# A list schedule with a shared port, a clock and a load pipe, a rank for each unit of work, and 1e-9 as a column of the sum

## The chip, the core and the metric

The kernel runs on one core of one Trainium2 chip. The metric is the device time of one execution in microseconds, the median over several runs. A profiled execution has a span besides, from the first to the last instruction that the profiler records; the device time is a little longer than the span.

The core's engines run side by side, each with its own queue of instructions in program order: PE (TensorE, matmuls), DVE (VectorE), ACT (ScalarE), POOL (GpSimd) and SP, which here only issues transfers between the chip's memory and the on-chip buffers. An instruction starts when those ahead of it on its engine allow it and the semaphores that it waits for are there. So the order within each queue is fixed when the program is built.

## The reference

Sparse attention of 8 batches, 8 heads, 576 positions and 64 columns per head feeds a gated layer of 512 columns:

```python
scores = scale * np.matmul(q, k.transpose(0, 1, 3, 2))
mask_local = (rel >= 0) & (rel < stride)                  # stride = 32, heads 0 to 3
mask_strided = (rel >= 0) & (pos[None, :] % stride == pos[:, None] % stride)   # heads 4 to 7
scores = np.where(masks[None, :, :, :], scores, -1000000000.0)
scores = scores - np.max(scores, axis=-1, keepdims=True)
attn = np.exp(scores)
attn = attn / (np.sum(attn, axis=-1, keepdims=True) + 1e-09)
x = np.matmul(attn, v)                                    # heads side by side: (8, 576, 512)
xp = np.concatenate([np.zeros((B, K - 1, D)), x], axis=1)
for k in range(K):                                        # K = 5
    gate_pre += conv_w[k][None, None, :] * xp[:, k:k + S, :]
gate = 1.0 / (1.0 + np.exp(-gate_pre))
val = x @ w_val
return (gate * val @ w_out).astype(np.float32)
```

The three weights arrive as float64; the kernel gets their bits and makes float32 values of them on the chip.

## The kernel before, in words

**Units of work.** For each batch b there are: three units of local attention (L, u = 0 to 2, two blocks of 96 positions each), two of strided attention (S, u = 0 and 1), four splits of x into a high and a low part (X, one per 128 columns), four gates (G, one per 128 columns), eight value groups (V, four times 128 columns e in two halves hf of the 576 positions, 12 matmuls each, of high and low parts) and four or five projection groups (P, 128 rows each, 12 matmuls). A local unit goes so: scores on PE into one of two banks `s_ps`; the mask added and the rows' maximum taken on DVE; maximum subtracted on POOL; exponential on ACT (tile `SML`, or `SMS` for strided units); sum, addition of 1e-9 and reciprocal on DVE (columns of a small tile `ST`); multiplication on POOL into `PB`; transposes on PE; copies on ACT into `BDL`; matmuls with v on PE into `x_ps`; a copy on ACT into `xs`. The strided unit multiplies into `PS`, transposes on DVE (`PT`) and copies into `BDS` on ACT. In batch 0's local units PE adds the mask by a matmul, and DVE subtracts the maximum. There are four gate tiles for all batches: DVE makes the gate's convolution in four steps per tile, ACT the tanh, and for batch 0's first gate PE makes the convolution. After the value group DVE multiplies gate and value into `GV`, ACT and POOL make its high and low part `ghi` and `glo`, and the projection reads these.

**Weights.** w_val comes in four parts of 512 KB into the tiles `xs`, w_out in four parts into one tile `osb2` (so each w_out load can start only when DVE has read the part before). Each part takes four passes on DVE (TENSOR_SCALAR, three SCALAR_TENSOR_TENSOR, in the gate tiles for w_val and `w64` for w_out), two on ACT and one subtraction on POOL. The conv weights take four small steps on DVE.

**The planner.** The program isn't issued as it is written. Class `Plan` records each step with its engine, an estimated cost, a rank and the steps that it depends on, which it finds from overlapping tiles. `issue` then makes a list schedule: it takes the engine that can start earliest, and on it the step of lowest rank among those that are ready by the planner's clock, and calls the instruction there (line 140, so nearly every instruction of the program has line 140 in the profile). The estimated costs are formulas of the operand's size, and between engines the constants `LATENCY` and `TURN` are added. A rank is 100 times the batch plus a number from the tables `RL`, `RS`, `RG`, `RV`, `RP` (one number per batch), `RWL`, `RWV`, `RWO` (one per weight part) and `RZ`. Up to 40 us of planned time the planner puts idle matmuls on zeros into PE's gaps (line 255). Memsets are on line 265.

The three lines that the softmax ends with:

```python
dve(rank, V.tensor_reduce, out=st[:, 1, :n], in_=sm, axis=AX.X, op=ALU.add)
dve(rank, V.tensor_scalar, out=st[:, 1, :n], in0=st[:, 1, :n], scalar1=1e-9, scalar2=None, op0=ALU.add)
dve(rank, V.reciprocal, extra=0.052, out=st[:, 2, :n], in_=st[:, 1, :n])
```

Of the kernel before, what the change touches and what calls it, by code (L numbers as in the profile page):

```python
# [21 lines left out]
KC = 5  # L22
# [11 lines left out]
class Plan:  # L34
# [6 lines left out]
    def __init__(self, filler, until):  # L41
        self.filler, self.until, self.spare = filler, until, None
        self.steps = []
        self.writes = {}
        self.reads = {}
# [16 lines left out]
    def add(self, engine, cost, rank, calls):  # L62
# [22 lines left out]
        self.steps.append((engine, cost, rank, calls, deps))  # L85
        return i

    def issue(self):
# [7 lines left out]
        free = {"pe": 1.1, "pool": 1.07, "dve": 0.9, "act": 1.9, "sp": 1.68}  # L96
        open_ = {}
        for i, s in enumerate(steps):
            if not left[i]:
                open_.setdefault(s[0], []).append(i)  # L100
        done = 0
        end = 0.0
        live, clear = {}, {}
        while done < len(steps):
            best = None
            for engine, queue in open_.items():
                if not queue:
                    continue
                t0 = free.get(engine, 0.0)
                start = max(t0, min(ready[i] for i in queue))  # L110
                if best is None or start < best[0]:
                    best = (start, engine)
            start, engine = best
# [3 lines left out]
            _, cost, _, calls, _ = steps[pick]  # L117
            t0 = free.get(engine, 0.0)
            free[engine] = start + cost
            over = start + cost + self.LATENCY[engine]  # L120
            end = max(end, over)
            for j in users[pick]:
                same = steps[j][0] == engine
                ready[j] = max(ready[j], start + cost + self.TURN[engine] if same else over)
                left[j] -= 1
                if not left[j]:
                    open_.setdefault(steps[j][0], []).append(j)
            if engine == "pe" and start < self.until:
                idle = [t for t in self.spare if not live.get(t.name) and clear.get(t.name, 0.0) <= t0]
                if idle:  # L130
                    for _ in range(int((start - t0 - 0.1) / (0.216 if t0 > COLD else 0.45))):
                        self.filler(idle[0])
            if engine == "pe":
                live[calls[0][1]["out"].name] = len([j for j in users[pick] if steps[j][0] != "pe"])
            else:
                for name in {ap.name for _, kw in calls for ap in kw.values() if hasattr(ap, "name")}:
                    if name in live:
                        live[name] -= 1
                        clear[name] = max(clear.get(name, 0.0), over)
            got = [fn(**kw) for fn, kw in calls]  # L140
            LOG.append((engine, start, cost, steps[pick][2], calls, got, pick))
            done += 1
# [4 lines left out]
def tile_sparse_attention_moe(  # L147
# [20 lines left out]
    plan = Plan(None, WARM)  # L168
# [19 lines left out]
    def dve(rank, fn, fast=False, extra=0.0, **kw):  # L188
        n = max(size(kw[k]) for k in ("out", "in0", "in_") if k in kw)
        plan.add("dve", ((n / 2 if fast else n) + 66) / 960.0 + extra, rank, [(fn, kw)])  # L190

    def act(rank, fn, wait=0.0, **kw):
        plan.add("act", size(kw["out"]) / 1200.0 + 0.05 + wait, rank, [(fn, kw)])

    def gps(rank, fn, two=True, extra=0.0, **kw):
        plan.add("pool", size(kw["out"]) * (2.35 if two else 1.03) / 1200.0 + 0.07 + extra, rank, [(fn, kw)])

    def pe(rank, each, calls):
        plan.add("pe", each * len(calls), rank, calls)
# [4 lines left out]
    def load(rank, out, in_):  # L204
        n = out.ap[0][1] * size(out)
        plan.add("sp", max(n * 4 / 360e3, 0.5), rank, [(nc.sync.dma_start, dict(out=out, in_=in_))])
# [56 lines left out]
    def zero(engine, rank, ap):  # L263
        eng = V if engine == "dve" else G
        plan.add(engine, size(ap) / (960.0 if engine == "dve" else 1200.0) + (0.02 if engine == "dve" else 0.035), rank, [(lambda out: eng.memset(out, 0.0), dict(out=ap))])

    def keep(rank, ap, step, base, sign):
        gps(rank, G.affine_select, False, extra=0.067, out=ap, in_=ap, pattern=[[step, ap.ap[1][1]]], compare_op=ALU.is_ge,
            fill=NEG, base=base, channel_multiplier=sign)

    for j in range(2):
        zero("dve", -9, KBL[:, j, :, :])
    zero("dve", -9, qSs[:, 2 * S:])


    zero("pool", -9, maskL[:, :])
    zero("pool", -9, maskS[:, :])
    for g in range(4):
        keep(-9, maskL[32 * g:32 * g + 32, :], 1, -1, -1)
        keep(-9, maskL[32 * g:32 * g + 32, :], -1, 32, 1)  # L280
    gps(-9, G.tensor_copy, False, extra=0.6, out=maskF[:, :, :], in_=maskL[:, None, :].to_broadcast([P, 3, 64]))
    plan.add("pool", 0.1, -9, [(lambda out: G.memset(out, NEG), dict(out=maskF[0:64, 0, 0:32]))])
# [345 lines left out]
```

## Time and profile before

| what | us (MB in the last row) |
|---|---|
| median of 3 runs | 349.1 (348.87 to 351.06) |
| the profiled execution | 349.0 |
| its span | 347.2 |
| PE busy | 313.3 (90%) |
| DVE busy | 261.3 (75%) |
| ACT busy | 222.8 (64%) |
| POOL busy | 211.1 (61%) |
| bytes read from and written to HBM | 33.84 and 9.44 MB |

How to read it: the rows with shares give the time in which each engine had an instruction running. A busy PE isn't PE at its peak, since a matmul at a lower clock is busy for longer; the clock that was granted stands in the windows' column PEclk (1.00 is full). In a group of instructions the columns are line, engine, operation, output and inputs with their sizes, the count, then busy time and mean nanoseconds of one, then the idle time just before them and what ended it. In a row of the timeline the start and the duration come first, and brackets give the idle time before it and what ended it. A wait's row gives the sum, how often, and the longest.

### The profile page before, as it was taken

The page shows a single profiled execution, that of the slowest core. Times are in us where ns is not written, and L with a number is a line of the kernel's source. Part 1 is how long each engine was busy: PE and PEld are TensorE (multiplying, and loading weights), DVE is VectorE, ACT ScalarE, POOL GpSimd, SP SyncE. Part 2 cuts the span into 40 slices and gives each one's busy share as a digit, 9 for nine tenths or more (in the row PEclk, how much of TensorE's full clock was granted, in tenths as well). Part 3 has the DMA queues.
Part 4 walks back from the last instruction along what each step waited for, and adds up shares of the span by engine and source line. Part 5 has one row for each costly group of instructions (what it writes and reads, how often), then busy time and mean ns, then how long its engine had stood idle before and what let it go on. Part 6 is the DMA issues. An engine that isn't in the chain of part 4 may idle for free.

```text
span 347.2 us, 9442 instructions
## 1 busy us (share of the span) xinstructions
PE 313.3 (90%) x3851; PEld 264.6 (76%) x3856; DVE 261.3 (75%) x447; ACT 222.8 (64%) x469; POOL 211.1 (61%) x248
## 2 busy tenths in 40 slices
PE   6879469788986999999999999999998999899995
PEld 2456358677875887898878988888898889888984
DVE  7786699999998599669837992979799945976200
ACT  7368666867857758547597747597469735764221
POOL 8676568878838835837458922976387805581510
PEclk9869989989999999999999999999999999999999
DMA  7965947625066406510456013923341031002012
GB/s 270 310 181 184 312 142 223 192 80 163 33 184 201 140 30 167 203 46 25 175 150 205 2 62 127 325 73 85 124 140 45 25 114 42 1 26 97 2 60 91
DMA packets 23419, 43.88 MB, mean 126 GB/s; under 512 B 3088, under 2 KB 13072, under 8 KB 22800
## 3 DMA queue, kind: packets, MB, share of 16 engines
q1 hardware_dynamic: 23376, 43.28, 39.5%
q8 instruction: 30, 0.49, 0.6%
q14 instruction: 13, 0.11, 0.1%
HBM read 33.84 MB, written 9.44 MB: 125 GB/s over the span
## 4 chain that ended last, share of the span: by engine, by line
PE 43%; DVE 26%; ACT 12%; POOL 8%; issue 5%; DMA 4%; SPq 1%; POOLq 0%; ACTq 0%; DVEq 0%
PE m_ps L140 35%; DVE gate L140 12%; DVE ST L140 7%; PE x_ps L140 4%; POOL PB L140 3%; PE s_ps L140 3%; ACT BDS L140 3%; DMA KBS<-in_kS_dram 3%; POOL xlo L140 3%; ACT BDL L140 2%; DVE w L140 2%; ACT gate L140 2%; PE t_ps L140 2%; DMA KBL<-in_kL_dram 2%; POOL PS L140 2%
## 5 line engine op out<-in xcount | busy, mean ns | idle before, releaser
L140 DVE SCALAR_TENSOR_TENSOR gate<-xs,cw,gate 128x576 f32<-128x576 f32 x124 | 126.0, 1035 | 10.4 <-ACT gate L140 9.3
L140 PE MATMUL m_ps<-xhi,wv 128*128 128x288 f32 x512 | 107.3, 303 | 4.9 <-DVE GV L140 4.9
L140 PE MATMUL m_ps<-wo,ghi 128*128 128x512 f32 x288 | 89.5, 392 | 0.0
L140 PEld LDWEIGHTS m_ps<-xhi,wv 128*128 128x128 f32 x512 | 82.0, 189 | 8.7 <-DVE GV L140 6.0
L140 POOL TENSOR_TENSOR glo<-GV,ghi 128x288 fp32r<-128x288 f32 x64 | 60.7, 956 | 43.3 <-ACT ghi L140 42.7
L140 PE MATMUL m_ps<-xlo,wv 128*128 128x288 f32 x256 | 76.0, 297 | 0.0
L140 POOL TENSOR_TENSOR xlo<-xs,xhi 128x576 fp32r<-128x576 f32 x32 | 49.5, 1564 | 27.7 <-ACT xhi L140 15.3
L140 PEld LDWEIGHTS m_ps<-wo,ghi 128*128 128x128 f32 x288 | 53.3, 188 | 11.0
L140 PE MATMUL m_ps<-wo,glo 128*128 128x512 f32 x144 | 56.4, 391 | 0.0
L140 PEld LDWEIGHTS m_ps<-xlo,wv 128*128 128x128 f32 x256 | 48.5, 189 | 0.0
L140 ACT CAST ghi<-GV 128x288 fp32r<-128x288 f32 x64 | 27.3, 432 | 24.6 <-DVE GV L140 24.2
L140 DVE SCALAR_TENSOR_TENSOR GV<-gate,m_ps 128x288 f32<-128x288 f32 x64 | 28.2, 441 | 13.5 <-PE m_ps L140 11.8
L140 ACT ACTIVATE gate<-gate 128x576 f32<-128x576 f32 x31 | 21.3, 686 | 26.4 <-DVE gate L140 26.3
L140 POOL TENSOR_TENSOR PB<-SML,ST 128x256 f32<-128x256 f32 (+1 forms) x48 | 30.4, 647 | 10.6 <-DVE ST L140 6.8
L140 ACT COPY xs<-x_ps 128x288 f32<-128x288 f32 (+1 forms) x56 | 32.0, 597 | 7.4 <-PE x_ps L140 7.4
L140 ACT ACTIVATE osb<-m_ps 128x512 f32<-128x512 f32 x36 | 21.0, 592 | 18.2 <-PE m_ps L140 16.1
L140 ACT COPY BDL<-t_ps 64x256 f32<-64x256 f32 (+1 forms) x72 | 26.6, 370 | 8.3 <-PE t_ps L140 7.3
L140 PEld LDWEIGHTS m_ps<-wo,glo 128*128 128x128 f32 x144 | 27.0, 188 | 6.2 <-POOL glo L140 0.6
L140 ACT COPY BDS<-PT 32x288 f32<-32x288 f32 x64 | 27.7, 433 | 5.6 <-DVE PT L140 4.6
L140 DVE TENSOR_REDUCE ST<-SML 128x6 f32<-128x384 f32 x45 | 24.1, 540 | 6.7 <-ACT SML L140 6.3
L140 PE MATMUL x_ps<-BDS,vSs 128*64 128x72 f32 x512 | 21.4, 236 | 5.5 <-ACT BDS L140 4.6
L140 PEld LDWEIGHTS x_ps<-BDS,vSs 128*64 128x64 f32 x512 | 18.5, 142 | 10.0 <-ACT BDS L140 6.1
(83 smaller groups left out, 421.0 us busy)
## 6 DMA issues: line engine op xcount, KB each, us to landing
out_dram<-osb SPq DMA_DIRECT2D x36, 256.0 KB
qLs<-in_qL_dram SPq DMA_DIRECT2D x16, 288.0 KB
KBL<-in_kL_dram SPq DMA_DIRECT2D x16, 288.0 KB
vLs<-in_vL_dram SPq DMA_DIRECT2D x8, 576.0 KB
qSs<-in_qS_dram SPq DMA_DIRECT2D x16, 288.0 KB
KBS<-in_kS_dram SPq DMA_DIRECT2D x16, 288.0 KB
vSs<-in_vS_dram SPq DMA_DIRECT2D x32, 128.0 KB
xs<-in_w_val_dram SPq DMA_DIRECT2D x4, 512.0 KB
```

What stands on the lines that cost most here:

```text
L140: got = [fn(**kw) for fn, kw in calls]
```

## The change

It has three parts.

**The planner's model.** `LATENCY` and `TURN` go. A step on DVE or POOL that uses the port which both share now waits for the other engine's last such step, less `PORT`. PE has a clock: in windows of 3.413 us its busy share decides whether the next matmuls count 1.9 times as long. A load takes 0.6 on SP, and its bytes go through one pipe for all loads at 330 KB per us. On ACT a step whose output begins on another partition than the one before begins after that one's end. An engine is free again a little before a step's end (`EARLY`). The steps' costs are new numbers. No instruction is added by this part, except that the number of idle matmuls comes from it.

**Ranks.** Every unit of work has a name (`L3.1`, `V1.2.0`, `load qS4`, `make wo2`), 270 in all, and one number in the table `RANK`. The old tables go. `ONPE` names the same three units as before, and `HELD` is empty, so its branch isn't taken.

**1e-9.** `SML` is 65 columns wide instead of 64, `SMS` 19 instead of 18; four memsets on POOL write 1e-9 into the added columns once; the sum runs over the wide tile; and the 40 additions on DVE go (24 of 6 columns, 16 of 16).

```diff
-    LATENCY = {"pe": 0.2, "dve": 0.15, "act": 0.14, "pool": 0.1, "sp": 0.95}
-    TURN = {"pe": 0.0, "dve": 0.12, "act": 0.15, "pool": 0.1, "sp": 0.0}
+    AFTER = {"pe": 0.045, "dve": 0.05, "act": 0.05, "pool": 0.04, "sp": 0.05}
+    EARLY = {"pe": 0.07, "dve": 0.08, "act": 0.1, "pool": 0.04, "sp": 0.0}
+    PORT = {"dve": 0.19, "pool": 0.14}
+    WINDOW, QUIET, BUSY, SLOW = 3.413, 0.48, 0.85, 1.9
+    ISSUE, TO_DATA, TO_END = 0.6, 1.2, 0.65
...
-            pick = min((i for i in queue if ready[i] <= start + 1e-9), key=lambda i: (steps[i][2], i))
+            pick = min((i for i in queue if ready[i] <= start + 1e-9), key=lambda i: (rank[steps[i][2]], i))
...
+            if engine == "pe":
+                fill = 0
+                idle = [t for t in self.spare if not live.get(t.name) and clear.get(t.name, 0.0) <= t0]
+                if idle and start < WARM:
+                    fill = max(0, int((start - t0 - 0.1) / (0.216 if warm else 0.45)))
+                    for _ in range(fill):
+                        self.filler(idle[0])
+                now = int(start / self.WINDOW)
+                spent = fill * (0.216 if warm else 0.45)
+                while window < now:
+                    full = min(1.0, (busy + min(spent, self.WINDOW)) / self.WINDOW)
+                    spent = max(0.0, spent - self.WINDOW)
+                    warm = full >= self.QUIET if warm else full >= self.BUSY
+                    window, busy = window + 1, max(0.0, busy - self.WINDOW)
...
+            elif engine == "sp":
+                free[engine] = start + self.ISSUE
+                pipe = max(pipe, start + self.TO_DATA) + took
+                done = pipe + self.TO_END
+            else:
+                if where != part[engine]:
+                    start = max(start, over[engine] + 0.015)
+                part[engine] = where
+                done = start + took
+                if shared:
+                    wait = max(0.0, port - start - self.PORT[engine])
+                    done += wait
+                    port = done
+                free[engine] = done - early
...
-    SML = Ring(tiles(2, [P, 2, 3, 64], "SML"))
+    SML = Ring(tiles(2, [P, 2, 3, 65], "SML"))
-    SMS = Ring(tiles(2, [P, 16, NT], "SMS"))
+    SMS = Ring(tiles(2, [P, 16, NT + 1], "SMS"))
...
+    for t in SML.items:
+        zero("pool", "zero SML", t[:, :, :, 64:65], 1e-9)
+    for t in SMS.items:
+        zero("pool", "zero SMS", t[:, :, NT:], 1e-9)
...
+        sm = whole[:, :, :w]
...
-        dve(rank, V.tensor_reduce, out=st[:, 1, :n], in_=sm, axis=AX.X, op=ALU.add)
-        dve(rank, V.tensor_scalar, out=st[:, 1, :n], in0=st[:, 1, :n], scalar1=1e-9, scalar2=None, op0=ALU.add)
-        dve(rank, V.reciprocal, extra=0.052, out=st[:, 2, :n], in_=st[:, 1, :n])
+        dve(group, V.tensor_reduce, out=st[:, 1, :n], in_=whole, axis=AX.X, op=ALU.add)
+        dve(group, V.reciprocal, extra=0.0055 * n, out=st[:, 2, :n], in_=st[:, 1, :n])
...
-RL = [-25.55, -293.34, -91.63, -48.77, -38.39, -126.5, -119.7, -85.3]
+RANK = [
+    53, 94, 159, 161, 120, 116, 124, 125, 131, 160, 39, 99, 216, 3, 158, 28, 228, 70, 82, 152, 80, 201, 34, 249,
```

**Where instructions move.** The new line of the issuing call is 171 instead of 140. The first place is DVE's start. `gate0` and `gate1` hold the weight part in work, `xs0` and `xs1` its raw bits (parts 0 and 1 in `xs0`, 2 and 3 in `xs1`); `s_ps` are batch 0's first scores. Before:

```order
L140 TENSOR_SCALAR gate1_93<-xs0_77 128x512
L140 SCALAR_TENSOR_TENSOR gate1_93<-xs0_77,gate1_93 128x512 x2
L140 TENSOR_SCALAR gate0_92<-xs0_77 128x512
L140 SCALAR_TENSOR_TENSOR gate1_93<-gate3_95,gate1_93 128x512
L140 SCALAR_TENSOR_TENSOR gate0_92<-xs0_77,gate0_92 128x512 x2
L140 SCALAR_TENSOR_TENSOR gate0_92<-gate2_94,gate0_92 128x512
L265 MEMSET xs0_77 128x4x4
L140 TENSOR_REDUCE ST0_108<-s_ps0_117 128x6
L140 TENSOR_TENSOR SML0_102<-s_ps0_117,ST0_108 128x3x2x64
```

and in the change, from part 1's last pass on:

```order
L171 SCALAR_TENSOR_TENSOR gate1_93<-gate3_95,gate1_93 128x512
L171 TENSOR_SCALAR gate0_92<-xs1_78 128x512
L171 TENSOR_SCALAR w640_115<-cw64_91 128x20
...
L171 TENSOR_SCALAR gate1_93<-xs1_78 128x512
...
L171 SCALAR_TENSOR_TENSOR cw_90<-w641_116,w640_115 128x20
L171 SCALAR_TENSOR_TENSOR gate1_93<-gate3_95,gate1_93 128x512
L171 TENSOR_SCALAR w640_115<-osb2_114 128x512
L171 TENSOR_REDUCE ST0_108<-s_ps0_117 128x6
L171 TENSOR_REDUCE ST1_109<-s_ps1_118 128x6
```

All four parts of w_val and the conv weights now stand ahead of the first reduction of scores; before, two parts did. On PE 65 idle matmuls stand ahead of the first scores instead of 16, and 25 later in both, so 90 in all instead of 41.

The second place is DVE in the middle of batch 1's softmaxes, between passes over w_out in `w640`. Before:

```order
L140 TENSOR_REDUCE ST1_109<-SML1_103 128x6
L140 TENSOR_REDUCE ST2_110<-SML0_102 128x6
L140 TENSOR_SCALAR ST1_109<-ST1_109 128x6
L140 TENSOR_TENSOR SMS0_106<-s_ps0_117,maskS_66 128x288
L140 RECIPROCAL ST1_109<-ST1_109 128x6
L140 TENSOR_SCALAR ST2_110<-ST2_110 128x6
L140 TENSOR_REDUCE ST0_108<-SMS0_106 128x16
L140 RECIPROCAL ST2_110<-ST2_110 128x6
```

and in the change:

```order
L171 SCALAR_TENSOR_TENSOR w640_115<-w641_116,w640_115 128x512
L171 TENSOR_REDUCE ST1_109<-SML1_103 128x6
L171 RECIPROCAL ST1_109<-ST1_109 128x6
L171 STREAM_TRANSPOSE PT0_101<-PS1_100 128x512
L171 TENSOR_REDUCE ST2_110<-SML0_102 128x6
L171 TENSOR_TENSOR SML1_103<-s_ps1_118,maskL_64 128x3x2x64
L171 RECIPROCAL ST2_110<-ST2_110 128x6
L171 TENSOR_TENSOR SMS0_106<-s_ps0_117,maskS_66 128x16x18
```

The reciprocal follows the sum without an addition between. The row that writes `SMS0` is batch 1's first strided unit S1.0 in both; in the change 14 instructions stand between the last pass that reads part wo1 out of `osb2` and this row.

The third place is SP's queue of loads. Before:

```order
L140 DMA osb2_114<-in_w_out_dram 128x4x256
L140 DMA qLs_71<-in_qL_dram 64x1152 x2
L140 DMA KBL_73<-in_kL_dram 64x2x576 x2
L140 DMA osb2_114<-in_w_out_dram 128x4x256
L140 DMA vLs_75<-in_vL_dram 96x6x256
L140 DMA vLs_75<-in_vL_dram 32x5x256
L140 DMA qSs_72<-in_qS_dram 64x1152 x2
L140 DMA KBS_74<-in_kS_dram 64x1152 x2
```

and in the change:

```order
L171 DMA qLs_71<-in_qL_dram 64x1152
L171 DMA KBL_73<-in_kL_dram 64x2x576 x2
L171 DMA osb2_114<-in_w_out_dram 128x4x256
L171 DMA vSs_76<-in_vS_dram 2x2048 x2
L171 DMA qLs_71<-in_qL_dram 64x1152
L171 DMA vSs_76<-in_vS_dram 2x2048
L171 DMA qSs_72<-in_qS_dram 64x1152
L171 DMA KBS_74<-in_kS_dram 64x1152 x2
L171 DMA osb2_114<-in_w_out_dram 128x4x256
L171 DMA qSs_72<-in_qS_dram 64x1152
```

The two halves of a load of q were neighbours; now a part of w_out and other loads stand between them, three times in the program: for batch 1's local and strided q and for batch 3's local q.

More of the change, by code (lines that the diff above doesn't have):

```diff
@@ L60, in _meet, with add @@
         return a[0] < b[1] and b[0] < a[1] and a[2] < b[3] and b[2] < a[3]
-    def add(self, engine, cost, rank, calls):
+    def add(self, engine, took, group, calls, port=False, early=None, part=0):
         i = len(self.steps)
@@ L84, in add, with issue @@
             self.writes.setdefault(name, []).append((i, boxes))
-        self.steps.append((engine, cost, rank, calls, deps))
+        self.steps.append((engine, took, group, calls, deps, port, self.EARLY[engine] if early is None else early, part))
         return i
-    def issue(self):
+    def issue(self, rank):
         steps = self.steps
@@ L103, in issue @@
+        port = pipe = end = 0.0
+        warm, window, busy = True, 0, 0.0
         live, clear = {}, {}
[L104 to L113, printed above, removed]
+        for _ in steps:
+            start, engine = min((max(free[e], min(ready[i] for i in open_[e])), k) for k, e in enumerate(self.ENGINES) if open_[e])
+            engine = self.ENGINES[engine]
@@ L114, in issue @@
             queue = open_[engine]
-            pick = min((i for i in queue if ready[i] <= start + 1e-9), key=lambda i: (steps[i][2], i))
+            pick = min((i for i in queue if ready[i] <= start + 1e-9), key=lambda i: (rank[steps[i][2]], i))
             queue.remove(pick)
[L117 to L121, printed above, removed]
+            _, took, _, calls, _, shared, early, where = steps[pick]
@@ L122, in issue @@
+            over[engine] = done
+            end = max(end, done)
             for j in users[pick]:
-                same = steps[j][0] == engine
-                ready[j] = max(ready[j], start + cost + self.TURN[engine] if same else over)
+                ready[j] = max(ready[j], done + (0.035 if steps[j][0] == engine else self.AFTER[engine]))
                 left[j] -= 1
                 if not left[j]:
[L127 to L132, printed above, removed]
+                    open_[steps[j][0]].append(j)
@@ L138, in issue @@
                         live[name] -= 1
-                        clear[name] = max(clear.get(name, 0.0), over)
+                        clear[name] = max(clear.get(name, 0.0), done)
             got = [fn(**kw) for fn, kw in calls]
-            LOG.append((engine, start, cost, steps[pick][2], calls, got, pick))
-            done += 1
+            LOG.append((engine, start, took, steps[pick][2], calls, got, pick))
         return end
@@ L261, in tile_sparse_attention_moe, with zero @@
     make_identity(nc, ident)
[L263 removed]
+    def zero(engine, group, ap, value=0.0):
         eng = V if engine == "dve" else G
[L265 to L268 removed]
+        plan.add(engine, size(ap) / (1170.0 if engine == "dve" else 1200.0) + 0.1, group,
+                 [(lambda out: eng.memset(out, value), dict(out=ap))])
@@ L269, in keep @@
+    def keep(group, ap, step, base, sign):
+        gps(group, G.affine_select, 0.001, extra=0.17, out=ap, in_=ap, pattern=[[step, ap.ap[1][1]]], compare_op=ALU.is_ge,
             fill=NEG, base=base, channel_multiplier=sign)
     for j in range(2):
[L272 to L277, printed above, removed]
+        zero("dve", "zero KBL", KBL[:, j, :, :])
+    zero("dve", "zero KBL", qSs[:, 2 * S:])
+    zero("pool", "mask L", maskL[:, :])
@@ L278, in tile_sparse_attention_moe @@
+    zero("pool", "mask L", maskS[:, :])
     for g in range(4):
[L279 to L282, printed above, removed]
-    act(-9, A.copy, out=maskLB[:, :], in_=maskL[:, :])
-    act(-9, A.copy, out=maskFB.rearrange("p k w -> p (k w)"), in_=maskF.rearrange("p k w -> p (k w)"))
@@ L314, in from_f64 @@
+        dve(group, V.scalar_tensor_tensor, out=t if whole is None else whole, in0=u, scalar=LEAST, in1=t,
             op0=ALU.is_ge, op1=ALU.mult)
```

314 lines of the change are left out of this document (166 added, 148 removed), and 11 rows, old and new, of the table RANK.

## The prediction

> **What bounds the kernel now.** I read the page of the profile first, then the busy time of each engine in stretches, then the waits of PE and DVE, and last the groups of instructions that the change touches.
>
> ```profile
> span 347.2 us, 9442 instructions
> PE 313.3 (90%) x3851; PEld 264.6 (76%) x3856; DVE 261.3 (75%) x447; ACT 222.8 (64%) x469; POOL 211.1 (61%) x248
> PE 43%; DVE 26%; ACT 12%; POOL 8%; issue 5%; DMA 4%; SPq 1%; POOLq 0%; ACTq 0%; DVEq 0%
> ```
>
> PE is busy for 90% of the span, yet the chain that ended last runs through DVE for 26%. Two engines bound the kernel at different times. The stretches show where one hands over to the other; their bounds are the first scores (9.24), the middle of the attention of the first batches (54.6), the first value group of batch 1 that is behind everything (111.7), and the last stretches of PE.
>
> ```profile
> core 0: us, PE busy (x) PEld busy (x) DVE busy (x) ACT busy (x) POOL busy (x), PEclk, DMA share, GB/s
> 0.00:9.24 9.24, 6.03 (x16) 2.11 (x17) 6.99 (x13) 7.14 (x12) 8.03 (x24) 1.00 0.79 276
> 9.24:54.60 45.36, 34.91 (x663) 24.64 (x668) 35.89 (x73) 28.03 (x64) 30.83 (x35) 0.85 0.73 217
> 54.60:111.70 57.10, 47.08 (x730) 40.85 (x725) 55.67 (x96) 42.82 (x94) 41.81 (x46) 0.97 0.51 158
> 111.70:145.40 33.70, 31.56 (x328) 26.99 (x325) 27.87 (x45) 24.01 (x51) 21.35 (x26) 1.00 0.43 135
> 145.40:329.70 184.30, 179.94 (x2065) 158.98 (x2066) 134.42 (x222) 117.42 (x247) 107.78 (x120) 1.00 0.28 90
> 329.70:347.20 17.50, 13.77 (x62) 11.06 (x60) 0.45 (x1) 3.42 (x6) 1.26 (x2) 1.00 0.20 75
> ```
>
> From 54.6 to 111.7 DVE is busy for 55.67 of 57.10 us and PE for 47.08 with 0.97 of its clock: DVE bounds. From 111.7 on PE is busy for 31.56 of 33.70 and then 179.94 of 184.30, and DVE has room: PE bounds. The hand-over is seen in single rows:
>
> ```profile
> 109.97 0.56 DVE L140 TENSOR_TENSOR SML<-s_ps,maskL 128x384 f32<-128x384 f32 x1
> 110.58 0.77 PE L140 MATMUL s_ps<-KBS,qSs 128*32 128x36 f32 x64 [1.49 <-DVE SML L140]
> 111.70 0.51 PE L140 MATMUL m_ps<-xhi,wv 128*128 128x288 f32 x2
> ```
>
> PE waits 1.49 us until DVE has read a score bank, writes batch 3's strided scores, and begins the value group of batch 1 (gate tile 2, first half) that I call M. From here PE hardly stops. So the time is that of M plus what PE has left, and the time of M is what DVE must do ahead of it, plus DVE's idle time. DVE was busy for 6.99 + 35.89 + 55.67 = 98.55 us by then, and idle for 111.70 - 98.55 = 13.15.
>
> **Term A: DVE's work ahead of M.** I counted DVE's instructions ahead of M's place in both orders. The change has 11 additions of 1e-9 on 6 columns and 7 on 16 columns less (those of this part of the program; the other 22 lie where PE bounds), and the new order has 2 steps of the gate's convolution, one transpose, one sum over SMS and 2 reciprocals of 16 columns fewer, but 2 reductions of SML, one GV and one reciprocal of 6 more.
>
> ```profile
> L140 DVE SCALAR_TENSOR_TENSOR gate<-xs,cw,gate 128x576 f32<-128x576 f32 x124 | 126.0, 1035 | 10.4 <-ACT gate L140 9.3
> L140 DVE TENSOR_SCALAR ST<-ST 128x6 f32<-128x6 f32 x24 | 12.3, 512 | 0.2
> L140 DVE TENSOR_SCALAR ST<-ST 128x16 f32<-128x16 f32 x16 | 4.3, 270 | 0.1
> L140 DVE STREAM_TRANSPOSE PT<-PS 128x512 f32<-128x512 f32 x16 | 11.3, 706 | 6.2 <-POOL PS L140 5.6 <-ACT BDS L140 0.3
> L140 DVE TENSOR_REDUCE ST<-SMS 128x16 f32<-128x288 f32 x32 | 13.9, 442 | 3.9 <-ACT SMS L140 3.6
> L140 DVE TENSOR_REDUCE ST<-SML 128x6 f32<-128x384 f32 x45 | 24.1, 540 | 6.7 <-ACT SML L140 6.3
> L140 DVE SCALAR_TENSOR_TENSOR GV<-gate,m_ps 128x288 f32<-128x288 f32 x64 | 28.2, 441 | 13.5 <-PE m_ps L140 11.8 <-POOL glo L140 1.7
> L140 DVE RECIPROCAL ST<-ST 128x6 f32<-128x6 f32 x24 | 4.4, 182 | 0.3
> L140 DVE RECIPROCAL ST<-ST 128x16 f32<-128x16 f32 x16 | 3.9, 242 | 0.2
> ```
>
> At these means the additions are worth 11 x 0.512 + 7 x 0.270 = 7.5 us, the other parts fewer 2 x 1.035 + 0.706 + 0.442 + 2 x 0.242 = 3.7, those more 2 x 0.540 + 0.441 + 0.182 = 1.7: together 9.5 less. But an addition on 6 columns doesn't cost 0.512 by itself:
>
> ```profile
> 45.59 0.13 DVE L140 TENSOR_SCALAR ST<-ST 128x6 f32<-128x6 f32 x1
> 56.82 0.79 DVE L140 TENSOR_SCALAR ST<-ST 128x6 f32<-128x6 f32 x1
> ```
>
> The same work takes 0.13 us or 0.79. The long ones stand still for something else, and I read that as DVE waiting for POOL, which is in the middle of a long operation. Where this wait is for POOL's work, the next DVE operation may have to wait it out instead. With 0.15 each, the additions are worth 18 x 0.15 = 2.7 and the term 4.7. I have no row that tells how much of the wait is passed on, and take the middle, **7.1 us less**, with 4.7 and 9.5 as its bounds. The sums now run over 65 and 19 columns for 64 and 18, which is 1.5% and 5.5% of 0.540 and 0.442 at most, under 0.03 each, and nothing in the sum.
>
> The Trainium skill, "VectorE: DVE Perf Modes", section "The TRN2 errata — SBUF-src ops pay a fixed extra latency per instruction", gives an operation of VectorE within SBUF a fixed 58 cycles of 0.96 GHz on top of its elements. As an estimate from that page an addition on 6 columns costs about 0.06 us, 18 of them 1.2, and the time by it would be about 343 us. The trace disagrees: its shortest such row has 0.13, twice that, so the measurement decides.
>
> **Term B: DVE's idle time ahead of M.**
>
> ```profile
> DVE SML L140 <- PE s_ps L140: 2.4, 1, 2.4
> DVE ST L140 <- PE s_ps L140: 2.1, 2, 1.4
> DVE ST L140 <- ACT SMS L140: 1.7, 2, 1.0
> DVE gate L140 <- ACT gate L140: 1.2, 1, 1.2
> ```
>
> Of the 13.15 us about 2.1 come before the first weight is there (the first stretch has 9.24 - 6.99 = 2.25) and stay. 4.5 are waits for the first scores and for a score bank; in the new order 65 idle matmuls stand ahead of PE's first scores instead of 16, and the scores are asked for later, so DVE reaches them after PE has. But the start gets a new wait:
>
> ```profile
> 1.19 6.03 PE L255 MATMUL m_ps<-idle 128*128 128x512 bf16 x16 [1.19 <-DVE none L258]
> 4.49 0.51 DVE L140 TENSOR_SCALAR gate<-xs 128x512 uint32<-128x512 uint32 x1 [0.78 <-DMA xs<-in_w_val_dram]
> 8.89 0.69 DVE L140 SCALAR_TENSOR_TENSOR gate<-gate,gate 128x512 f32<-128x512 f32 x1
> 11.02 0.56 DVE L140 TENSOR_REDUCE ST<-s_ps 128x6 f32<-128x384 f32 x1 [1.41 <-PE s_ps L140]
> 12.08 2.50 POOL L140 TENSOR_TENSOR wv<-gate,wv 128x512 fp32r<-128x512 f32 x2
> 14.07 2.97 PE L255 MATMUL m_ps<-idle 128*128 128x512 bf16 x13
> L140 DVE TENSOR_SCALAR w<-cw 128x20 uint32<-128x20 uint32 x1 | 1.2, 1242 | 0.0
> L140 DVE TENSOR_SCALAR w<-osb 128x512 uint32<-128x512 uint32 x4 | 4.1, 1036 | 0.7 <-POOL wo L140 0.7
> L265 POOL MEMSET maskS<- 128x18 f32 x1 | 0.1, 114 | 0.0
> ```
>
> DVE makes w_val parts 0 and 1 from 4.49 to 9.58, as now. The next instruction in the new order makes part 2 in the tile gate0, which POOL must have read for part 0. POOL does that at 12.08 in the row, behind all its memsets; four small ones are added ahead (at most 4 x 0.114, I take 0.36), so it ends at 12.08 + 0.36 + 2.50 / 2 = 13.7. DVE is idle for 13.7 - 9.58 = 4.1. Behind it DVE can't run ahead: scores and all else are queued after this instruction. Of the rest, 13.15 - 2.1 - 4.5 = 6.5, I leave 5: the new order puts more unlike units next to each other, so a sum finds its exponential done more often. Idle becomes 2.1 + 4.1 + 5 = 11.2, **1.9 us less**; bounds: 6.8 less (the start's wait is filled and half of the rest goes), 2 more (all the rest stays, and a score bank waits as before).
>
> The many idle matmuls: 16 took 6.03 us while PE was cold, 13 took 2.97 later, 0.228 each. The 49 more end at 1.19 + 6.03 + 49 x 0.228 = 18.4, and the three local scores and masks follow in some 2.2 us (in the old order they begin at 9.24 and DVE's first reduction follows at 11.02; I add a little): 20.6. DVE meanwhile makes parts 2 and 3 (5.1, as 4.49 to 9.58), the conv weights (1.24 for the first of four steps, 2.7 for all) and starts w_out (1.04), from 13.7: 22.5. So the idle matmuls cost nothing, by 2 us. If they stay at 6.03 / 16 = 0.377 each, PE would be ready at 27.9, 5.4 late.
>
> **Term C: PE after M.** PE has 347.2 - 111.7 = 235.5 us left at M. Its work ahead of M is 0.7 us more in the new order, counted in units at the durations of full clock, so 0.7 less is left. Its idle time after M is (33.70 - 31.56) + (184.30 - 179.94) = 6.5 in the stretches above. I leave it as it is, since the same steps feed it; bounds 3 and 9.5. **0.7 us less.**
>
> **Sum.** M comes at 98.55 - 7.1 + 11.2 = 102.65, and 235.5 - 0.7 = 234.8 follow: a span of 337.5. The profiled execution took 349.0 with a span of 347.2, 1.8 around it: **339.3 us**, 9.7 or 2.8% less. The execution is as the median of the runs, 349.1, so nothing has to be shifted.
>
> **The rivals.**
>
> *No change.* The waits for POOL are passed on whole (A -4.7), the start's wait comes on top (B +2) and PE's stalls after M grow to 9.5 (C -0.7 + 3): 349.0 - 4.7 + 2 + 2.3 = 348.6. For it speaks that POOL is busy for 41.81 of the 57.10 us where DVE bounds, against it that fewer instructions stand in the chain of each softmax.
>
> *More.* The additions are worth their means (A -9.5), the better fit of units takes the other idle time (B -6.8) and half of PE's (C -0.7 - 3.5): 328.5. For it speaks the clock of 0.85 in the second stretch, which more idle matmuls could lift; against it that DVE's idle time before M is already only 13.15 in all.
>
> *Slower: loads that stand behind a weight.* SP's queue is one line. In the new order the part wo1 is queued ahead of the second half of batch 1's local q, wo2 ahead of that of its strided q, wo3 ahead of batch 3's local q. Each w_out load waits until DVE has read the part before out of osb2, and all loads behind it wait too.
>
> ```profile
> 34.88 8.74 DMA KBS<-in_kS_dram
> PE s_ps L140 <- DMA KBS<-in_kS_dram: 5.1, 1, 5.1
> ```
>
> Take S1.0, batch 1's first strided scores. After the last step that reads osb2, DVE has 14 instructions until it needs these scores, 6.3 us by the rows above without the weight step among them. The two loads take 512 + 288 = 800 KB / 217 GB/s = 3.7 us at the second stretch's rate, or 8.74 like the row. Above 6.3 PE and DVE both wait. If all three places cost what the late KBS cost PE in the old order, 339.3 + 3 x 5.1 = 354.6.
>
> **How the numbers follow.** The forecast 0.57, own range 333 to 345.5. No change 0.16, more 0.16, slower 0.11 (one or two places alone, or the cold idle matmuls, end at 344.4 to 349.5, between the cases). A measurement of this kernel tells about 1% from no change, 3.5 us. Faster by over 1%: 0.57 + 0.16 = 0.73; within 1%: 0.16; slower: 0.11. The range goes from 329.5, near the end of "more", to 348, short of "no change" and "slower".
>
> **What would show it.** A: DVE's busy time falls by 17 us or less (12.3 + 4.3 are all the additions), by 7 to 10 ahead of M, and M begins near 102.7; if the waits are passed on, the mean of the reciprocals behind the sums rises over 0.18 and 0.24. B: DVE is idle from 9.6 to 13.7 for POOL's wv, and then not for PE before 22. C: PE's busy time after M is about 224.6 us (31.56 + 179.94 + 13.77 - 0.7), with 6 or 7 idle before the last stretch. Wrong would make it: PE waits of several us on the loads of q or KBS; DVE's idle time ahead of M above 15; M near 102 and yet a later end, which would mean that PE's stalls after M have grown.

## The result, and the profile after

The changed kernel takes **338.07 us** (median of 4 runs, 336.95 to 338.82) where the kernel before takes 349.0 beside it: a ratio of 0.967, with a 95% interval of 0.9625 to 0.9716. The forecast was 339.3. The profiled execution has a span of 336.5, 10.7 less than before. The first lines of its page and the shares of the chain that ended last:

```profile
span 336.5 us, 9465 instructions
PE 321.1 (95%) x3905; PEld 266.2 (79%) x3905; DVE 247.4 (74%) x407; ACT 222.7 (66%) x469; POOL 214.6 (64%) x252
PE 72%; DMA 8%; DVE 7%; POOL 4%; ACT 4%; SPq 2%; issue 2%; POOLq 0%; ACTq 0%; DVEq 0%
```

PE is busy for 95% and makes 72% of the chain, 43% before; DVE's share of it fell from 26% to 7%. Next the stretches around M, the value group V1.2.0 of batch 1, which the timeline shows at 104.42 us:

```profile
104.42 0.52 PE L171 MATMUL m_ps<-xhi,wv 128*128 128x288 f32 x2
```

```profile
core 0: us, PE busy (x) PEld busy (x) DVE busy (x) ACT busy (x) POOL busy (x), PEclk, DMA share, GB/s
0.00:54.60 54.60, 48.42 (x801) 29.32 (x801) 45.37 (x93) 37.57 (x81) 40.84 (x67) 1.00 0.87 263
54.60:104.42 49.82, 46.74 (x636) 40.80 (x637) 43.31 (x71) 34.52 (x73) 41.56 (x38) 0.93 0.46 140
104.42:336.50 232.08, 225.93 (x2471) 196.08 (x2469) 158.73 (x246) 150.63 (x316) 132.25 (x147) 1.00 0.32 97
```

Ahead of M, DVE is busy for 45.37 + 43.31 = 88.68 us, 9.9 less than before's 98.55, and idle for 104.42 - 88.68 = 15.74, 2.6 more. Behind M the program needs 232.1, 3.4 less than before's 235.5, with PE busy for 225.93, much as before (31.56 + 179.94 + 13.77 = 225.27): what went is PE's idle time. -9.9 + 2.6 - 3.4 gives the 10.7. (M is DVE's busy time plus its idle time whichever engine bounds, so this sum alone doesn't show that DVE does.) In the second stretch PE is now the busier engine, 46.74 of 49.82 us against DVE's 43.31. Before it was the other way round.

DVE's groups show what became of the additions' time:

```profile
L171 DVE SCALAR_TENSOR_TENSOR gate<-xs,cw,gate 128x576 f32<-128x576 f32 x124 | 128.0, 1066 | 7.4 <-ACT gate L171 7.0
L171 DVE RECIPROCAL ST<-ST 128x6 f32<-128x6 f32 x24 | 4.3, 180 | 0.2
L171 DVE RECIPROCAL ST<-ST 128x16 f32<-128x16 f32 x16 | 3.9, 244 | 0.1
```

The reciprocals behind the sums cost what they did (182 and 242 ns before), so the waits didn't pass on to them; the gate's steps cost 1066 ns for 1035, 2.0 us in all. DVE's busy time fell by 261.3 - 247.4 = 13.9, of the 12.3 + 4.3 = 16.6 that the additions took, but the order changed as well; e1 below tells how much passed on.

### The profile page after: what moved, and what is told of

It is laid out like the page before. It is cut to its first block, busy times and chain, and to the rows that moved or that the text cites. A ratio compares the mean times of both kernels' runs of the same rounds, so it can differ in the third digit from the quotient of the medians.

```text
span 336.5 us, 9465 instructions
## 1 busy us (share of the span) xinstructions
PE 321.1 (95%) x3905; PEld 266.2 (79%) x3905; DVE 247.4 (74%) x407; ACT 222.7 (66%) x469; POOL 214.6 (64%) x252
## 4 chain that ended last, share of the span: by engine, by line
PE 72%; DMA 8%; DVE 7%; POOL 4%; ACT 4%; SPq 2%; issue 2%; POOLq 0%; ACTq 0%; DVEq 0%
PE m_ps L171 54%; PE x_ps L171 10%; PE s_ps L171 6%; DMA out_dram<-osb 4%; PE t_ps L171 3%; DVE gate L171 3%; DMA vLs<-in_vL_dram 3%; SPq L171 2%; DMA osb<-in_w_out_dram 2%; DVE ST L171 1%; DVE w L171 1%; ACT BDS L171 1%; ACT osb L171 1%; POOL KBS L303 1%; ACT BDL L171 1%
## 5 line engine op out<-in xcount | busy, mean ns | idle before, releaser
L171 DVE SCALAR_TENSOR_TENSOR gate<-xs,cw,gate 128x576 f32<-128x576 f32 x124 | 128.0, 1066 | 7.4 <-ACT gate L171 7.0
L171 PE MATMUL m_ps<-xhi,wv 128*128 128x288 f32 x512 | 105.6, 300 | 2.1 <-DVE GV L171 1.7
L171 PE MATMUL m_ps<-wo,ghi 128*128 128x512 f32 x288 | 91.2, 398 | 0.0
L171 POOL TENSOR_TENSOR xlo<-xs,xhi 128x576 fp32r<-128x576 f32 x32 | 52.8, 1656 | 27.4 <-ACT xhi L171 26.9
L171 PEld LDWEIGHTS m_ps<-wo,ghi 128*128 128x128 f32 x288 | 52.3, 188 | 11.4 <-DVE gate L171 0.2
L171 ACT CAST ghi<-GV 128x288 fp32r<-128x288 f32 x64 | 27.5, 432 | 34.2 <-DVE GV L171 33.8
L171 ACT COPY xs<-x_ps 128x288 f32<-128x288 f32 (+1 forms) x56 | 32.5, 603 | 9.0 <-PE x_ps L171 8.4
L171 POOL TENSOR_TENSOR PB<-SML,ST 128x256 f32<-128x256 f32 (+1 forms) x48 | 32.6, 687 | 6.6 <-PE t_ps L171 3.7
L171 POOL TENSOR_TENSOR SML<-SML,ST 128x384 f32<-128x384 f32 x21 | 21.4, 1020 | 9.7 <-DVE ST L171 9.7
L171 DVE TENSOR_REDUCE ST<-SML 128x6 f32<-128x390 f32 (+1 forms) x45 | 24.2, 544 | 3.7 <-ACT SML L171 3.5
L171 PE MATMUL s_ps<-KBL,qLs 128*32 128x128 f32 x576 | 21.0, 282 | 4.9 <-DVE gate L171 2.8
```

## The experiments

Each run's median stands beside runs of the kernel before on the same chip in the same session, 349.0 to 349.7. PE's lag in the table below is worked out by me: a time t, less the work that PE had begun by then, each unit at its duration at full clock (a value group 1.60, a projection group 2.72, and so on); it grows when PE stands, runs at a low clock or runs idle matmuls. It is an estimate good to a few tenths: at the end before and the change differ by 11.0, their spans by 10.7.

| PE's lag, us, at | 30 | 50 | 60 | 70 | 110 | 180 | end |
|---|---|---|---|---|---|---|---|
| before | 19.5 | 28.3 | 30.6 | 33.9 | 42.0 | 45.5 | 51.2 |
| e1, old order without additions | 18.5 | 28.3 | 29.4 | 31.6 | 39.2 | 42.4 | 47.4 |
| the change | 23.1 | 26.3 | 32.1 | 33.6 | 34.4 | 35.6 | 40.2 |
| e2, new order with additions | 25.9 | 29.5 | 33.2 | 38.6 | 39.5 | 41.3 | 46.3 |
| e5, one load of w_out later | 23.1 | 26.1 | 30.8 | 31.6 | 32.5 | 33.8 | 38.2 |

**The additions and the order, apart.** In e1 the planner of the kernel before still plans the additions, but nothing is issued for them, so all other instructions keep their order:

```diff
-        dve(rank, V.tensor_scalar, out=st[:, 1, :n], in0=st[:, 1, :n], scalar1=1e-9, scalar2=None, op0=ALU.add)
+        dve(rank, lambda **kw: None, out=st[:, 1, :n], in0=st[:, 1, :n], scalar1=1e-9, scalar2=None, op0=ALU.add)
```

> The kernel before, in its own order on every engine, without the 40 additions: the sums run over 65 and 19 columns, and four memsets on POOL at the start write 1e-9 there. My theory (a good half of the gain is DVE time that the additions took ahead of M, the first value group behind the hand-over from DVE to PE): 349.0 falls by 18 additions at about 0.28, so to 344 us, with 341.5 to 346.5 as its bounds, and M comes about 5 us earlier. The rival (the order makes the gain, and the additions only stood where DVE waited for POOL anyway): 347.5 to 349.5, since the next DVE instruction waits instead.

It took 345.08 (344.73 to 347.03), a ratio of 0.989 (0.986 to 0.992).

```profile
core 0: us, PE busy (x) PEld busy (x) DVE busy (x) ACT busy (x) POOL busy (x), PEclk, DMA share, GB/s
0.00:54.60 54.60, 42.44 (x694) 26.85 (x695) 43.41 (x80) 36.21 (x77) 40.67 (x62) 0.91 0.75 230
54.60:108.37 53.77, 45.55 (x718) 39.51 (x716) 49.73 (x83) 41.89 (x90) 42.38 (x46) 0.97 0.52 162
108.37:343.40 235.03, 224.98 (x2451) 197.36 (x2449) 156.88 (x246) 144.08 (x303) 131.79 (x146) 1.00 0.30 96
```

DVE's work ahead of M falls by 98.55 - 43.41 - 49.73 = 5.4 us, M comes at 108.37 for 111.70, 3.3 earlier, and the rest after M stays at 235. So the removed time counts, at about six tenths of it. In the whole program DVE's busy time fell by 261.3 - 250.0 = 11.3 of the 16.6, so about a third of the additions' time came back in other instructions:

```profile
PE 313.0 (91%) x3856; PEld 263.7 (77%) x3856; DVE 250.0 (73%) x407; ACT 222.2 (65%) x469; POOL 214.9 (63%) x252
```

In e2 the changed kernel gets its additions back in the step of the sum:

```diff
-        dve(group, V.tensor_reduce, out=st[:, 1, :n], in_=whole, axis=AX.X, op=ALU.add)
+        total = st[:, 1, :n]
+        plan.add("dve", size(whole) / 960.0 + 0.143, group, [
+            (V.tensor_reduce, dict(out=total, in_=whole, axis=AX.X, op=ALU.add)),
+            (V.tensor_scalar, dict(out=total, in0=total, scalar1=1e-9, scalar2=None, op0=ALU.add))])
```

> The changed kernel in its own order on every engine, with the 40 additions put back, each right behind its sum (the extra column holds 0). My theory as the prediction had it (DVE sets the time of M): 338.1 rises by about 5, to 343 (340.8 to 345.6). The rival (in the new order PE is what bounds from 60 us on, and DVE was idle for 15.7 us ahead of M): it rises by 0 to 2, to 338 to 340.

It took 341.61 (339.83 to 344.4), 0.977 (0.973 to 0.980) of before: 3.5 more than the change, between the two expectations and inside the first. Directly behind its sum an addition takes less on 6 columns than before (0.512) and more on 16 (0.270):

```profile
L171 DVE TENSOR_SCALAR ST<-ST 128x6 f32<-128x6 f32 x24 | 7.9, 328 | 0.8
L171 DVE TENSOR_SCALAR ST<-ST 128x16 f32<-128x16 f32 x16 | 5.1, 321 | 0.6
```

So the additions are worth 3.9 us in the old order and 3.5 in the new, and the order the rest of the 10.9: 7.0 without them and 7.4 with them. The rival that the additions cost nothing falls in the old order. In the new one the intervals of e2 and of the change (0.963 to 0.972) don't meet, but e2's fastest execution, 339.83, lies where the rival had it, and the profiled one, 344.4, lost 2.4 us at its start by a hold of DVE that the last section shows; how much of the 3.5 is such a hold isn't known.

Where the order's 7 us lie is seen against e1, which differs from the change by the order and the idle matmuls alone. From 70 to 110 us PE falls back by 7.6 in e1 and by 0.8 in the change. From 75 to 105 PE is busy without a break in the change, and in e1 it stands before three instructions, by the profile 1.8 us for a bank of scores, 1.0 for a bank of values and 1.9 for the tile BDS (first row e1, second the change):

```profile
75.00:105.00 30.00, 26.05 (x308) 22.59 (x308) 28.36 (x45) 21.87 (x46) 21.51 (x21) 0.94 0.43 125
75.00:105.00 30.00, 30.00 (x387) 25.57 (x386) 28.41 (x47) 18.55 (x39) 26.90 (x25) 1.00 0.39 126
```

Which of the many exchanged units brings this is not shown.

**The idle matmuls.** e3 drops the first 49:

```diff
+    first = [i for i, (s, _) in enumerate(todo) if s is None][:49]
+    for i in first[::-1]:
+        del todo[i]
```

> The changed kernel with 16 idle matmuls ahead of the first scores instead of 65, all else in the same order. The prediction's reason (the 49 more are hidden, since DVE reaches the scores at 20.1 and PE had them at 19.3): no change, 337 to 339. The rival (they keep PE's clock up for what follows): the matmuls of the first scores and those behind them run at half clock, PE falls behind by 2 to 4 us before 45, and the time is 340 to 342.

It took 336.61 (333.14 to 337.32), a ratio of 0.962 (0.957 to 0.967): not slower, so the rival falls. Its timeline shows why PE had the time:

```profile
1.19 5.95 PE L304 MATMUL m_ps<-idle 128*128 128x512 bf16 x16 [1.19 <-DVE none L307]
15.07 2.79 PE L184 MATMUL s_ps<-KBL,qLs 128*32 128x128 f32 x48 [7.93 <-DMA KBS<-in_kS_dram]
17.79 0.50 PE L184 MATMUL s_ps<-maskFB,identB 128*128 128x384 bf16 x1
18.08 0.53 PE L184 MATMUL s_ps<-maskLB,identB 128*128 128x384 bf16 x1
```

Without the 49, PE stands for 7.93 us, by the profile for the load of KBS. These scores read KBL and q, and in the new order a part of w_out and a half of the strided q are queued ahead of the last half of q; that it is this half that they wait for is read from the queue and not shown. Then PE runs its first scores at a low clock (0.52 from 10 to 20 us, and 2.79 us for 48 matmuls, 1.52 in the change), and has the first two units' masks on at 18.6 where the change has 19.3. DVE comes for them at 20.1 in both.

**The late half of q.** The changed kernel's largest wait of PE lies at batch 3's first local scores:

```profile
PE s_ps L171 <- DVE gate L171: 2.8, 1, 2.8
```

```profile
54.78 0.88 PE L171 MATMUL x_ps<-BDL,vLs 128*64 128x96 f32 x16 [1.30 <-ACT BDL L171]
58.47 1.51 PE L171 MATMUL s_ps<-KBL,qLs 128*32 128x128 f32 x24 [2.81 <-DVE gate L171]
```

These scores read nothing that DVE's gate writes. e5 issues the load of wo3 behind the second half of batch 3's q. For that the planned steps are kept in a list `todo`, which is edited before it is issued; `at` finds a step in it:

```diff
+    def behind(group, name, nth, group2, name2, nth2):
+        step = todo.pop(at(group, name, nth))
+        todo.insert(at(group2, name2, nth2) + 1, step)
+
+    behind("load wo3", "sp", 0, "load qL3", "sp", 3)
```

> The changed kernel with one load moved: the fourth part of w_out (wo3) is issued behind the second half of batch 3's local q instead of ahead of it; all else in the same order. In the changed kernel's profile PE stands for 2.81 us ahead of the scores L3.0, and its clock is down for the 5 us behind. If the late q half is the cause (the prediction's rival on loads, at one of its three places): that wait falls below 1, and the time by 2 to 4, to 334 to 336. If the wait is for something else (the profile names DVE's gate as releaser): the wait stays and the time is 337 to 339.

```profile
54.26 0.88 PE L189 MATMUL x_ps<-BDL,vLs 128*64 128x96 f32 x16 [1.48 <-ACT BDL L189]
55.14 0.86 PE L189 MATMUL s_ps<-KBL,qLs 128*32 128x128 f32 x24
58.11 1.16 PE L189 MATMUL x_ps<-BDL,vLs 128*64 128x96 f32 x16 [2.11 <-ACT xs L189]
```

The scores now follow at once, at full clock. So the wait was for the load, and the named releaser was not its cause. But the next matmul stands for 2.11 us, by the profile for a bank that ACT has to copy out, so 0.7 us of the wait is won there, and PE's lag is 2.0 less at the end. The load also held up DVE, through PE: DVE's first GV waits for PE's first value group, 2.59 us in the change (1.61 in e3) and 0.40 in e5 and in e12 below, which moves the load too (the change, then e5):

```profile
66.64 0.46 DVE L171 SCALAR_TENSOR_TENSOR GV<-gate,m_ps 128x288 f32<-128x288 f32 x1 [2.59 <-PE m_ps L171]
66.31 0.45 DVE L189 SCALAR_TENSOR_TENSOR GV<-gate,m_ps 128x288 f32<-128x288 f32 x1 [0.40 <-PE m_ps L189]
```

In e5 M comes at 102.54, 1.9 earlier than in the change, with DVE idle for 12.7 us ahead of it. The median is 336.89 (335.26 to 337.9), the ratio 0.9645 (0.960 to 0.969). The interval overlaps that of the change; the time alone doesn't tell the 1.2 us from nothing.

**The start.** e9 puts POOL's work on the weights ahead of its memsets (`behind` is as in e5):

```diff
+    for n in (3, 2, 1, 0):
+        behind("load vS0", "sp", n, "make wv1", "pool", 0)
+    for n in range(2):
+        behind("zero PS", "pool", 0, "make wv1", "pool", 0)
+    for n in range(2):
+        behind("zero SMS", "pool", 0, "make wv1", "pool", 0)
+    behind("zero vSs", "pool", 0, "make wv1", "pool", 0)
```

> The changed kernel with POOL's two subtractions for the first two w_val parts ahead of the memsets of vSs, SMS and PS instead of behind them, and the first four loads into vSs behind that memset; all else in the same order. DVE then goes on with part 2 about 1.2 us earlier (11.7 for 12.88). If DVE's start is on the path (the prediction's term B): 1 to 1.5 us less, 336.5 to 337. If the loads and PE's stall near 58 set what follows: no change, 337.5 to 339.

It took 340.23 (339.64 to 340.96), a ratio of 0.973 (0.971 to 0.975), some 2 us more, which neither reason expected. DVE did go on at 11.62 for 12.88:

```profile
11.62 4.24 DVE L195 TENSOR_SCALAR gate<-xs 128x512 uint32<-128x512 uint32 x1 [1.43 <-POOL wv L195]
```

```profile
10.31 2.50 POOL L195 TENSOR_TENSOR wv<-gate,wv 128x512 fp32r<-128x512 f32 x2 [1.86 <-ACT wv L195]
12.74 1.81 POOL L326 MEMSET vSs<- 128x2048 f32 x1
14.49 0.18 POOL L326 MEMSET SMS<- 128x16 f32 x2
14.58 1.00 POOL L326 MEMSET PS<- 128x512 f32 x2
```

But its first instruction, 0.42 us when alone, lasts for 4.24, until POOL's unbroken row of instructions ends at 15.58. The wait for POOL turned into a long DVE instruction, 1.3 us won and some 2.8 lost (in the change the same instruction takes 1.47, 12.88 to 14.35, and here it ends at 15.86). That makes 1.5 of the 2 us; whether the moved loads into vSs cost something as well wasn't told apart.

**Model or ranks.** e4 has the new planner with the old ranks, e6 to e8 each leave one part out of its model, e10 and e11 only change one constant a little, as a control:

```diff
-    tile_sparse_attention_moe.end = plan.issue(dict(zip(names, RANK)))
+    tile_sparse_attention_moe.end = plan.issue({name: old_rank(name) for name in names})     # e4, e6, e7, e8, e10, e11
...
-    AFTER = {"pe": 0.045, "dve": 0.05, "act": 0.05, "pool": 0.04, "sp": 0.05}
+    AFTER = {"pe": 0.045, "dve": 0.05, "act": 0.05, "pool": 0.04, "sp": 0.95}                # e8
...
-                if shared:
+                if False:                                                                    # e6
...
-    WINDOW, QUIET, BUSY, SLOW = 3.413, 0.48, 0.85, 1.9
+    WINDOW, QUIET, BUSY, SLOW = 3.413, 0.48, 0.85, 1.0                                       # e7
...
-                pipe = max(pipe, start + self.TO_DATA) + took
-                done = pipe + self.TO_END
+                done = free[engine] = start + max(took * 330 / 360, 0.5)                     # e8
...
-    PORT = {"dve": 0.19, "pool": 0.14}
+    PORT = {"dve": 0.17, "pool": 0.14}                                                       # e10
...
-    ISSUE, TO_DATA, TO_END = 0.6, 1.2, 0.65
+    ISSUE, TO_DATA, TO_END = 0.6, 1.2, 0.75                                                  # e11
```

> The changed kernel's planner, with its new model of the port, the clock and the loads, its costs and the 1e-9 column, but each unit's rank is that of the kernel before (100 times the batch plus the old tables' number). If the model makes the order good, it comes near the change: 338 to 342. If the ranks make it: 343 to 350, where the kernel before without the additions is, or later, as old ranks and new model don't belong together.

> The planner of the changed kernel with the old ranks (run e4: 339.1), but its model leaves out the port that DVE and POOL share; all else as in e4. If this is the part of the model that makes the order good, 343 to 346 (the old order without the additions took 345.1); if not, 337.5 to 341.

> As e4, but the model's PE never slows (its matmuls count once, not 1.9 times, in cold windows); the idle matmuls are counted as in e4. If the clock in the model is what matters, 343 to 346; if not, 337.5 to 341. I expect no change, since the clock is low only before 75 us in the old order.

> As e4, but loads are modelled as in the kernel before: SP is taken for the time of the bytes at 360 KB per us, and the load is there 0.95 us later, with no pipe for all loads. My guess is that the load model matters most, since the 5.1 us wait for KBS of the old order is gone in e4: 342 to 346 if so, and 337.5 to 341 if not.

> A control for e6 to e8: as e4 (339.1), with the one constant PORT for DVE at 0.17 instead of 0.19. The order of about a third of DVE's instructions changes with it. If orders from nearly the same model scatter little, 337.5 to 341, and what e6 to e8 lost is due to the parts left out. If the scatter is as large as those losses: anywhere from 340 to 350, and e7 and e8 (345.9 and 345.2) show nothing by themselves.

> A second control of the same kind: as e4, with a load's landing (TO_END) at 0.75 instead of 0.65. Small scatter: 337.5 to 341; large: 340 to 350.

| run | median, us | runs from and to | ratio, 95% interval |
|---|---|---|---|
| e4, old ranks | 339.08 | 337.84 to 342.24 | 0.972 (0.967 to 0.978) |
| e6, no port | 358.23 | 354.66 to 360.03 | 1.022 (1.017 to 1.028) |
| e7, no clock | 345.94 | 344.09 to 349.70 | 0.989 (0.985 to 0.992) |
| e8, no load pipe | 345.22 | 344.54 to 346.37 | 0.989 (0.986 to 0.992) |
| e10, port 0.17 | 343.52 | 341.69 to 344.79 | 0.983 (0.978 to 0.987) |
| e11, landing 0.75 | 365.89 | 363.40 to 367.87 | 1.047 (1.041 to 1.052) |

e4 by itself would say that the model alone makes the order, and e6 that the port is the part that counts. The controls take both back. A landing of 0.75 us instead of 0.65 costs 26.8 us, more than any part left out, and a port constant of 0.17 instead of 0.19 costs 4.4. In e11 PE's largest wait is by the profile for w_out's conversion:

```profile
PE m_ps L171 <- ACT wo L171: 14.1, 1, 14.1
```

So nearly the same model with the same ranks gives orders from 339 to 366 us, and e4 was the best of three. These runs show neither that the model is worth the 7 us nor which part of it is; that the 270 ranks are is not shown either. What they show is that the order moves this program by over 25 us, and that with the same ranks a small change of one constant is enough for that. The new ranks were run with their own constants alone, so how much they depend on these isn't known.

**Both edits.** e12 joins e3 and e5, since each read below the change.

> The changed kernel with both edits that read below it before: 16 idle matmuls ahead of the first scores (336.6 alone) and the fourth part of w_out behind batch 3's q half (336.9 alone). If the two lie at different places and neither was chance: 338.1 - 1.5 - 1.2, so 335 to 336. If one of them was only the scatter of this order's runs (336.4 to 338.8): 336.5 to 338.

It took 335.96 (334.09 to 337.75, 6 runs), 0.960 (0.957 to 0.963) of before. That is where the first expectation had it and 2.1 us under the change's median, but the intervals overlap (0.9625 to 0.9634), so a small gain over the change is likely rather than shown. The six times form two groups, 334.1 to 334.9 and 337.0 to 337.8; the profiled one (337.5) had its start held as the last section tells, so the median may lie between two kinds of execution.

## Why the prediction was right, and where its terms were off

**The bound.** That DVE sets the time of M in the old order was right: e1 takes 5.4 us from DVE there and M moves by 3.3. That it would still do so in the new order was right only in part. From 54.6 us to M, PE is the busier engine, and DVE waits for it; but with the additions put back (e2) M comes at 109.40, 5.0 later, of which 2.4 are there at the start already, so DVE's time ahead of M still counts.

**Term A** was 7.1 less, bounds 4.7 to 9.5; it measured 9.9, a little beyond its far bound. Its larger part, 5.1 for the additions, measured 5.4 in e1, which leaves 4.5 for the order's part, 2.0 in the term. I had feared that the waits pass on to the next instruction. To the reciprocals they don't; in the whole program e1 got about a third of the additions' time back in other instructions, 1.4 us of it in the gate's steps. That the change's gate steps are longer by 2.0 us is no sign of it, since with the additions put back (e2) they take longer still, 1082 ns.

**Term B is the step that failed.** It had DVE's idle time ahead of M at 11.2, 1.9 less, and the last lines said that above 15 would make it wrong; it is 15.74, 2.6 more. The start went much as forecast: idle for 2.30 us until 12.88 where 4.1 until 13.7 was said, with a wait of 1.18 for ACT before it, and PE's first scores hidden behind DVE. But the rest of the idle time, for which I left 5, came to about 10, 4.6 of it in waits for PE and 1.8 for a part of w_out:

```profile
DVE GV L171 <- PE m_ps L171: 3.2, 3, 2.6
DVE gate L171 <- POOL wv L171: 2.3, 1, 2.3
DVE w L171 <- DMA osb<-in_w_out_dram: 1.8, 1, 1.8
DVE SMS L171 <- PE s_ps L171: 1.4, 2, 0.8
```

I had taken the old order's 4.5 us of waits for PE out and put none in for the new order. A load behind a weight I had priced as a rival only; it came about at batch 3's q, held PE and through it DVE, and with that one load moved (e5) the idle time is 12.7, so 3.1 of the missing 4.5 go with it. The miss reached M: A was 2.8 better, B 4.5 worse, and M 1.8 later than forecast (104.42 for 102.65).

**Term C** was 0.7 less and measured 3.4. The 0.7 less of PE's work doesn't show, since PE's busy time behind M is 0.7 more (225.93 for 225.27). I held PE's idle time after M at 6.5, "since the same steps feed it". It fell to (232.08 - 18.50) - (225.93 - 14.42) = 2.07 ahead of the last stretch, in which these rows show 14.42 of 18.50 busy:

```profile
318.00:336.50 18.50, 14.42 (x67) 11.72 (x65) 0.91 (x2) 3.84 (x7) 1.61 (x2) 1.00 0.19 72
```

e1's rest is 235.0 and e2's 233.2, so most of this comes with the order and not with the additions: the waits on x_ps that the old order has behind M are gone from the new one, where the two rows on m_ps are all that is left (before, then the change):

```profile
PE x_ps L140 <- ACT xs L140: 1.7, 3, 1.0
PE x_ps L140 <- ACT BDS L140: 1.5, 3, 0.7
PE x_ps L140 <- ACT BDL L140: 1.2, 3, 0.8
```

```profile
PE m_ps L171 <- DVE GV L171: 1.7, 3, 1.0
PE m_ps L171 <- ACT osb L171: 0.4, 1, 0.4
```

The two misses of M and of C nearly cancel, +1.8 and -2.7, and the sum came out 1.2 us from the time. The mechanism was right for the additions; for the order the total is right partly by luck.

**The rivals.** The slower one, loads behind a weight, is there at two of its three places: 2.81 us at batch 3's q and 0.84 at batch 1's local q. It was priced at 5.1 each.

```profile
31.90 1.52 PE L171 MATMUL s_ps<-KBL,qLs 128*32 128x128 f32 x48 [0.84 <-DMA qLs<-in_qL_dram]
```

Without the former (e5) another wait takes most of its place on PE. At S1.0, which I had taken as the likeliest, PE doesn't stand. There is a fourth place that neither the section on the change nor the prediction names: the first part of w_out stands ahead of the second half of batch 0's local q. If PE's wait of 7.93 us in e3 is for this half, that is what it costs PE there; in the change idle matmuls run in that time, and DVE comes for the scores later still. For "more" I had named the clock of 0.85, which more idle matmuls could lift; it is 1.00 up to 54.6 in the change, but e3, at 0.91, isn't slower.

**The page.** By the Trainium skill, "VectorE: DVE Perf Modes", section "The TRN2 errata — SBUF-src ops pay a fixed extra latency per instruction", the estimate for an addition was 0.06 us, and 343 for the time. Taken out, they moved the time by 3.9, three times the 1.2 that its figure makes of 18. The same section adds that its row comes out too short and that the fixed term measured there is near 150 cycles; as an estimate that makes 0.16 us of an addition and 3 us of 18, still less than the 5.4 of e1.

## What to carry to other kernels

Remove small instructions on the engine that bounds at that place, and price them by the time that the engine holds them, waits for a shared resource included; in e1 six tenths of the time that DVE won ahead of M came through to M. Before a gain is given to a planner's new model, disturb one of its constants by a tenth or two: if the time moves by more than the gain, the gain belongs to the one order that was found, and the model isn't shown to have made it. A wait removed by moving a transfer or a memset is worth what the next wait leaves of it, so read the next wait first.

## What the runs showed of the hardware

A TENSOR_SCALAR on DVE can be held by POOL for as long as POOL's instructions follow each other without a gap. The first weight pass of part 1, 0.43 us in the change's execution, took 4.68 in e2's, with the same instructions ahead of it on both engines (the change's row, then e2's, then POOL's in e2):

```profile
6.21 0.43 DVE L171 TENSOR_SCALAR gate<-xs 128x512 uint32<-128x512 uint32 x1
```

```profile
6.50 4.68 DVE L171 TENSOR_SCALAR gate<-xs 128x512 uint32<-128x512 uint32 x1
```

```profile
5.98 2.06 POOL L303 MEMSET KBS<- 128x1152 f32 x2
7.98 0.99 POOL L303 MEMSET PS<- 128x512 f32 x2
8.92 0.15 POOL L303 MEMSET SML<- 128x6 f32 x2
8.99 1.80 POOL L303 MEMSET vSs<- 128x2048 f32 x1
10.73 0.18 POOL L303 MEMSET SMS<- 128x16 f32 x2
```

It began at 6.50 and ended at 11.18, 0.27 behind the last memset of the row at 10.91; in e9 and in e12 (below) the end lies 0.28 behind. In e2 POOL's first memset of KBS (5.98) came ahead of DVE's pass (6.50); in the change the pass (6.21) came ahead of the memset (6.41). The two SCALAR_TENSOR_TENSOR passes right ahead of it took 1.42 in both, in e2 beside that memset, so not every DVE instruction is held. e12 has the hold too, e3 hasn't, and their orders are the same up to there:

```profile
6.64 3.94 DVE L192 TENSOR_SCALAR gate<-xs 128x512 uint32<-128x512 uint32 x1
```

So it is a matter of who comes first by a few tenths. Part 2 of w_val, for which DVE waits for ACT and POOL anyway, begins 2.4 us later in e2 than in the change (15.27 for 12.88) and 1.7 later in e12 than in e3 (14.68 for 12.94). That may be why the new order's runs spread more (e2: 339.8 to 344.4) than those of before; with one trace of each kernel that isn't shown. The Trainium skill, "SBUF — State Buffer", section "SBUF: two separate sides", says that DVE and GpSimd share a pair of ports as an exclusive lock which the one that starts first holds for its whole instruction. The trace agrees that DVE stands still, and shows more than one instruction's length: 4.68 and 4.24 us are several memsets in a row.
